# Retention and two MLPs on one core: absolute decays under one causal mask, four transposes in place of four loads, and a new order

## The chip, the cores and the metric

The kernel runs on one core of a Trainium2 chip. The metric is the device time of one execution in microseconds (us), the median of several. Smaller is better.

## What is computed

`q`, `k` and `v` have 2 batches, 8 heads, 768 tokens and 64 features per head. A decaying state runs over the tokens, and its output goes through two MLPs with 512 features in and out and 2048 in between.

```python
gamma = 1.0 - 2.0 ** (-5.0 - np.arange(H))
for t in range(S):
    state = gamma * state + k[t] (outer) v[t]
    y[t] = 1/sqrt(D) * q[t] @ state
x = y, as (1536 tokens, 512)
h = x @ w_in
g = (a0 + a1*h + a2*h**2 + a3*h**3) / (1 + |b0|*|h| + |b1|*h**2 + 1e-6)
x = g @ w_out
h = x @ w_in2
out = (h * sigmoid(h)) @ w_out2
```

## The kernel before

The host lays the data out first. `qt` and `kt` hold `q` and `k` with the features on the partitions, `k` and `v` hold them with the tokens on the partitions, and `consts` and `decays` hold powers of gamma.

**Chunks.** The retention is cut into 12 chunks of 128 tokens (2 batches times 6 positions; chunk c has position c // 2 and batch c % 2). For each chunk `attention` loads qT, kT, vn and kn (256 KB each) and does the following. TensorE forms the scores from kT and qT (`sc`). VectorE multiplies them by a mask (`am`). TensorE multiplies the masked scores by vn (`outs`), and from position 1 on adds qT times the running state `bd` to the same bank. `grow` forms kn times vn, which is added to `bd`. ScalarE and VectorE split the output into a high part `xh` and a low part `xl`. The decay within a chunk lies in the mask `msk` (512 KB, one matrix of 128 x 128 for each head, already causal). The decay between chunks lies in kn, which is multiplied by a power of 1/gamma (`cst`), and in qT, which from position 1 on is multiplied by a power of gamma (`gq`, loaded) after the scores have been taken.

**MLPs.** Four chunks make one group of 512 tokens; there are three groups. A step multiplies a group by 128 columns of w_in (12 matmuls of 512 columns, `mm_in`), runs a chain of elementwise operations on ScalarE and VectorE, splits the result into `gh` and `gl`, and multiplies by 128 rows of w_out (four times 3 matmuls, `mm_out`). The first steps belong to the first group and the first MLP, and run while chunks 4 to 11 are still in work. The weights are loaded raw (512 KB each, a ring of three `raw` buffers), rebuilt by two ScalarE operations and one VectorE operation into `wt`, and split into high and low parts `ih`, `il` (w_in) and `oh`, `ol` (w_out), the high one on ScalarE and the low one on GpSimd. Further groups use the weights in SBUF or load them back from a spill.

**Order.** Every operation is recorded with the cells that it reads and writes (`op`). `Flow.order` then emits all of them in the order that the table `ORDER` (a packed list of numbers) lists, so each engine's queue and the one DMA queue on SP hold what that table says. Engines and queues run in that order and wait on semaphores. The numbers in `R` were used to find orders; a few of them set other things, such as which chunks' scaling runs on VectorE (`kd`, `scp`: chunks 0 to 3) and which on GpSimd.

**Helpers.** Most elementwise operations are recorded by `act`, `tt`, `stt` and `ts`, so all have the lines of those helpers, and the operation is told by its tiles. Loads and stores are recorded by `dma`.

Of the kernel before, what the change touches and what calls it, by code (L numbers as in the profile page):

```python
# [15 lines left out]
AF = mybir.ActivationFunctionType  # L16
ALU = mybir.AluOpType

P = 128
# [4 lines left out]
R = {'lw': -463.92, 'T0': 689.59, 'tau0': 13.93, 'tau1': 122.19, 'c0': -129.63, 'dc': 67.51, 'conv': 39.61, 'half': 427.29, 'absl': -34.77, 'raw': 455.03, 'ret': 752.06, 'spl': -417.39, 'hi': 301.24, 'lo': 31.56, 'inn': -277.93, 'later': -32.81, 'split': -554.53, 'out': 359.39, 'evac': -363.13, 'qload': -20.08, 'scl': 238.79, 'sc': 858.37, 'am': -44.15, 'gr': 112.48, 'av': -547.62, 'bd': 198.47, 'xh': -201.14, 'xl': 110.32, 'glp': 48, 'lop1': 24, 'lop2': 30, 'scp': 4, 'ps': 17, 'ksc': 103.89, 'qa': -467.29, 'ka': 0, 'late': 20, 'mid': 4, 'pev': -317.29, 'pld': -385.01, 'cg': -489.85, 'wm': 11, 'mk': 26.43, 'ck': 21.3, 'g2': (1, 0, 2), 'ch0': 269.21, 'ch1': -102.81, 'ch2': 64.3, 'ch3': 22.33, 'ch4': -52.46, 'ch5': 5.42, 'ch6': -78.23, 'ch7': 237.84, 'ch8': 90.06, 'ch9': -61.88, 'ch10': -106.39, 'ch11': -212.52, 'ru0': 218.22, 'lu0': -107.8, 'ru1': 40.68, 'lu1': -106.06, 'ru2': 91.09, 'lu2': 146.01, 'ru3': -37.17, 'lu3': -39.51, 'rhalf': 125.38, 'wsum': 20.0, 'kd': 4, 'hb': 20}  # L24
# [7 lines left out]
    'c-jru0~-+L8UWDO@0VM)wrp!*aoNVQ?G_f6ZQHiBY}>Z6g{`{xSDfcWgQ$Q2a15fu50D5F0|P+>hzyY+BE*DP5F27ZTu2UaAPO9Z6L1oe!cIsJ=^',  # L32
    'zPYgM5%5_Cp592n8TBB!FG88<Ign_z_aT9!LpUAv<J&c(51ZLmEg6r=buOhF{<($OJjzAf$rSZ~$_^At(X`ArIt*BTyPj!Ou_@DuF;5s0(L7;Xh#',
    'f3(CVjI0NONG8~0^Pz*}Kc{m5TAU70+3Qz?qLRF{%-{310hZ68B7*vA`P!p=dcW_V)AovWP!waYlwV)0}#9q)E4nqrQ39X<5{D7z63S5J$fN1y<U',
    'PEN855GY}AZ!D@p%FBI#?S+P#*5GsuER~Z1x=tS+<<1#93o-B+i(Y7K@@xgZ{ZzWf|wWs+d@0I3+>?^+=urN0XxEF=medi8$`ngP!J1XEbIbZp*z',
    'IG_?Q4cKq2e{MG>$xI*x(gAu3LV;qW*71I6(n^n;HO9TQ_hOoYWS36{mASO)vTAMg|&!4pV_8L$LChJWER^oLLI1qMJl%#6QaGE9!YVtR~&m2e6S',
    'g&|NFdt+=Ih{Iqy6v0v$7b{>Dtc)ozBmRgrF$-43fshFYL00?;|AfIX60%_}tc}?*2j;}S*avgrAp8?YLp`j6^>GyZfpu{(4#$#M9v8znTnbgG8Z',
    'LopkP=70Sjdg3FfF#i*7zH?!8AAyQe#_ekNvR$HpKBT0XkqioCMWzD0ajV*a`DvUd)GiZ~)GLiZ~1>!$g<~jj%CJ#m+b$o8U;CfYWd~&W0}76}w?',
    'm?2a{X4lKu&xB^GvM4Sb)a0brA**FKAV>4`lbD<^n#Cfm=SK(Tmi}P?kF2Do08rR`uT#p-YBhH6ScnQZ~HCl)Zp*k&q8ng&D<3T)xNAWNo!{2ckj',
    'K=j)n^r;t+5nSq2=>Eu(2S<w7F>jv@d_Tn<5-94(kd8>jpzh6q!!eiuHy>0fmd-k)T5Jl3QuEWYDw4dCf>px*bA57VqA)=VFzx-C%6o6;~l(<XK*',  # L40
    'KO!<zIIpJRPm1NZP5zQC9G3fIC}tVQ?nH~NDA;lKD5zvDUFjpuPMKE#bMmUiKGoJo`EHNL@bxCh74J{(VP5$GKvy+@+WFo7=MMQla0XexccEzp|&',
    '#>n&lnS_**&?bmVKhRcqjQjB~oKHqmXg2MDC^V6h(KMPv(I^HbrRfx%V$vi0h@bE?{z%E`CyGU}DGtS@6LgMJP)ce-3n>+)rZg0fPSOl=nnX=0K1',
    'HB^Fbgf93v`~+(jvM@5vd4eqpXyZvQsYF2B+vW<)ETeoVG(c%1wD_F6E_sl%LYm6$+e)5>g}zl$a7wM#?~KC^KcE#Z-(+QVF_7SLqV{N~P#J{Y<5',
# [34 lines left out]
class Cell:  # L78


    bank = None
# [53 lines left out]
def retention_two_mlps(  # L135
# [114 lines left out]


    cst = Buf("cst", [P, NGAM])
    msk = Buf("msk", [P, 2, HP, P])
    gk = cst.t[:].rearrange("p (c h) -> p c h", h=H)
    par = Buf("par", [P, 14])
    ab, na, b1, b0, lb = par.t[:, 0:6], par.t[:, 6:10], par.t[:, 10:11], par.t[:, 12:13], par.t[:, 13:14]
    cq = par.t[:, 11:12]

    cqc, lbc, table = Cell(), Cell(), Cell()

    class Parted:

# [56 lines left out]
    def heads(t):  # L319
        return t[:].rearrange("p (a t) -> p a t", a=HP)  # L320
# [103 lines left out]
    def attention(c, s_banks, o_banks):  # L424
# [13 lines left out]
        if grows:  # L438

            if c < R["ka"]:  # L440

# [498 lines left out]
```

## Time and profile before

| | |
|---|---|
| median of 3 runs | 581.77 us (580.83 to 584.45) |
| profiled execution, its own time | 583.26 us |
| its span in the profile | 581.5 us |
| TensorE matmul busy | 567.3 us, 98% |
| VectorE, ScalarE, GpSimd busy | 427.6, 405.2, 174.2 us |
| DMA | 86.81 MB, mean 149 GB/s |

The span runs from the first to the last instruction of the profiled execution, and all places below are given in us from its start. A busy share is an average over stages with different limits: matmuls are pipelined and their records overlap, so 98% doesn't mean that TensorE is at its peak all the time. What is idle, and what the clock was, is read stage by stage.

### The profile page before, as it was taken

Reading aid. Unit: us, or ns where it says so; the run is one execution under the profiler, and the core shown is the slowest. Engines: PE = TensorE matmul, PEld = TensorE weight load, DVE = VectorE, ACT = ScalarE, POOL = GpSimd, SP = SyncE. Lnnn points to the kernel's source line nnn. Section 1 sums busy time; section 2 is a strip of 40 time slices with the busy share of each in tenths; the row PEclk is TensorE's granted clock in tenths of the full one; section 3 lists DMA queues with packets and bytes.
Section 4 is the critical chain, followed back from the end, with each engine's and each line's share of the span. In section 5 each row is a group of like instructions: output and inputs, shape, how many; then the busy total and the mean of one; then the engine's idle time right before and its main releaser. Section 6 shows DMA issues by size and latency. Waiting matters only on the chain.

```text
span 581.5 us, 8229 instructions
## 1 busy us (share of the span) xinstructions
PE 567.3 (98%) x2902; PEld 467.4 (80%) x2902; DVE 427.6 (74%) x673; ACT 405.2 (70%) x697; POOL 174.2 (30%) x141
## 2 busy tenths in 40 slices
PE   7879999999999999999999999999999999999997
PEld 6767777888888888888888888888888888888885
DVE  3878888798788887798878566578887888663331
ACT  2577988999988887787998888776634545334432
POOL 0435545534644523553463653310000000000000
PEclk8997999999999999999999999999999999999999
DMA  8999856443123310032044667865433422116811
GB/s 299 304 386 312 276 165 235 144 144 112 36 76 106 104 42 20 0 92 90 19 162 147 217 218 246 280 212 167 139 98 108 146 73 91 54 38 207 278 57 73
DMA packets 42585, 86.81 MB, mean 149 GB/s; under 512 B 4656, under 2 KB 4656, under 8 KB 42544
## 3 DMA queue, kind: packets, MB, share of 16 engines
q1 hardware_dynamic: 42544, 86.29, 44.5%
q8 instruction: 23, 0.38, 0.3%
q14 instruction: 18, 0.15, 0.1%
HBM read 65.30 MB, written 20.97 MB: 148 GB/s over the span
## 4 chain that ended last, share of the span: by engine, by line
PE 92%; DMA 3%; ACT 1%; issue 1%; DVE 1%; SPq 1%; POOL 1%; POOLq 0%; DVEq 0%; ACTq 0%
PE acc L603 45%; PE h L550 19%; PE a L550 10%; PE h L766 7%; PE a L766 7%; DMA raw<-in_moe_w_in_dram 2%; PE a L513 1%; DMA qT<-in_qt_dram 1%; PE a L503 1%; PE a L458 1%; SPq L362 1%; PE a L491 1%; PE acc L458 0%; POOL kn L336 0%; ACT wt L328 0%
## 5 line engine op out<-in xcount | busy, mean ns | idle before, releaser
L336 POOL TENSOR_TENSOR gl<-s,gh 128x512 fp32r<-128x512 f32 x48 | 62.7, 1307 | 111.6 <-ACT gh L328 74.8
L603 PE MATMUL acc<-gh,oh 128*128 128x512 f32 x192 | 75.8, 395 | 0.0
L603 PE MATMUL acc<-gl,oh 128*128 128x512 f32 x192 | 74.8, 390 | 0.0
L603 PE MATMUL acc<-gh,ol 128*128 128x512 f32 x192 | 74.8, 389 | 0.0
L603 PE MATMUL acc<-oh,gh 128*128 128x512 f32 x192 | 74.7, 389 | 0.0
L603 PE MATMUL acc<-oh,gl 128*128 128x512 f32 x192 | 74.7, 389 | 0.0
L603 PE MATMUL acc<-ol,gh 128*128 128x512 f32 x192 | 74.7, 389 | 0.0
L550 PE MATMUL h<-xh,ih 128*128 128x512 f32 x168 | 66.3, 395 | 0.0
L550 PE MATMUL h<-xh,il 128*128 128x512 f32 x168 | 65.7, 391 | 0.0
L550 PE MATMUL h<-xl,ih 128*128 128x512 f32 x168 | 65.7, 391 | 0.0
L414 POOL TENSOR_TENSOR il<-wt,ih 128x512 fp32r<-128x512 f32 x36 | 47.1, 1317 | 48.4 <-ACT ih L409 46.2
L343 DVE SCALAR_TENSOR_TENSOR wt<-wt,raw 128x512 int32<-128x512 int32 x64 | 46.2, 732 | 19.9 <-ACT raw L328 12.4
L414 POOL TENSOR_TENSOR ol<-wt,oh 128x512 fp32r<-128x512 f32 x36 | 47.6, 1325 | 29.0 <-ACT oh L409 24.5
L328 ACT ACTIVATE raw<-raw,par 128x512 int32<-128x512 uint32 x64 | 48.3, 759 | 6.1 <-DMA raw<-in_moe_w_in_dram 5.0
L343 DVE SCALAR_TENSOR_TENSOR s<-s,par,h 128x512 f32<-128x512 f32 x65 | 48.2, 744 | 1.2
L328 ACT ACTIVATE wt<-raw 128x512 f32<-128x512 f32 x64 | 42.2, 660 | 6.4 <-DMA raw<-in_moe_w_out_dram 4.0
L603 PEld LDWEIGHTS acc<-gh,oh 128*128 128x128 f32 x192 | 36.0, 188 | 7.8
L603 PEld LDWEIGHTS acc<-oh,gh 128*128 128x128 f32 x192 | 36.0, 188 | 7.5
L603 PEld LDWEIGHTS acc<-gl,oh 128*128 128x128 f32 x192 | 36.0, 188 | 7.5
L603 PEld LDWEIGHTS acc<-oh,gl 128*128 128x128 f32 x192 | 36.0, 188 | 7.5
L603 PEld LDWEIGHTS acc<-ol,gh 128*128 128x128 f32 x192 | 36.0, 188 | 7.4
L328 ACT ACTIVATE gh<-s 128x512 fp32r<-128x512 f32 x56 | 35.0, 626 | 9.9 <-PE acc L603 3.7
(249 smaller groups left out, 1292.0 us busy)
## 6 DMA issues: line engine op xcount, KB each, us to landing
raw<-in_moe_w_out_dram SPq DMA_DIRECT2D x32, 512.0 KB, 4.4
raw<-in_moe_w_in_dram SPq DMA_DIRECT2D x32, 512.0 KB, 4.7
spill<-wt SPq DMA_DIRECT2D x48, 256.0 KB, 4.7
wt<-spill SPq DMA_DIRECT2D x48, 256.0 KB, 2.9
qT<-in_qt_dram SPq DMA_DIRECT2D x12, 256.0 KB, 5.7
kT<-in_kt_dram SPq DMA_DIRECT2D x12, 256.0 KB, 5.9
vn<-in_v_dram SPq DMA_DIRECT2D x12, 256.0 KB, 5.9
kn<-in_k_dram SPq DMA_DIRECT2D x10, 256.0 KB, 6.1
```

Source lines behind the costliest of these rows:

```text
L328: lambda: nc.scalar.activation(out=out_, in_=in_, func=func, **kw),
L336: op(eng, dur, rank, lambda: e.tensor_tensor(out=out_, in0=in0, in1=in1, op=alu), reads, writes, port)
L343: lambda: nc.vector.scalar_tensor_tensor(out=out_, in0=in0, scalar=scalar, in1=in1, op0=op0, op1=op1),
L362: op("swdge" if swdge else "sync", us, rank, lambda: e.dma_start(out=out_, in_=in_), reads, writes)
L414: e.tensor_tensor(out=sl.t[nm + "l"][:, us], in0=wt.t, in1=sl.t[nm + "h"][:, us].bitcast(F32), op=ALU.subtract)
L458: nc.tensor.matmul(heads(sb_[j].t)[:, hp, :], kT.t[js, hp, :], qT.t[js, hp, :], start=True, stop=True)
L491: nc.tensor.matmul(st.t[j * D : (j + 1) * D, hp * D : (hp + 1) * D], kn.t[:, 2 * hp + j, :], vn.t[:, 2 * hp + j, :], start=(hp == 0), stop ...
L503: nc.tensor.matmul(heads(xo.t)[j * D : (j + 1) * D, hp, :], vn.t[:, 2 * hp + j, :], heads(am[j].t)[:, hp, :], start=(hp == 0), stop=not mo ...
L513: nc.tensor.matmul(heads(xo.t)[:, hp, :], old.t[:, hp, :], qT.t[:, hp, :], start=False, stop=True, skip_group_check=True,)
L550: nc.tensor.matmul(h.t, sl.t[w][:, ws], x[g].t[:, c, :], start=(n == 0), stop=(n == 3 * KD - 1))
L603: nc.tensor.matmul(a.t, a1, a2, start=(first and n == 0), stop=(last and n == 2))
L766: nc.tensor.matmul(b_.t, w[0](c, wlo), x[0](c, xlo), start=(start and n == 0), stop=(n == 5), skip_group_check=True)
```

## The change

The decay within a chunk no longer lies in the mask. Scores are now taken from a qT that has already been multiplied by an absolute power of gamma, at position 0 too, and vn, not kn, is multiplied by the power of 1/gamma (in all 12 chunks, before in 10). The mask is then one causal matrix of ones, the same for all heads. It is made on chip from 128 columns of the constants (`cst` grows from 24 KB to 88 KB), and an identity is made from it. The 512 KB load of `msk` is gone. The powers for position 0 come as two rows of 512 numbers, which a matmul with ones spreads over the partitions into the bank `acc3` (`spread`). The six MLP parameters come as two loads into one partition, and a matmul with ones spreads them too (`params`).

For chunks 0 to 3 kT is no longer loaded. TensorE transposes kn (four transposes of 128 x 128, line 448 of the changed kernel) into a score bank, and ScalarE copies the bank to the kT buffer. `ORDER` is a new table over the new list of operations; beyond the first two fifths of TensorE's queue the two orders run alike.

```diff
-    cst = Buf("cst", [P, NGAM])
-    msk = Buf("msk", [P, 2, HP, P])
...
+    cst = Buf("cst", [P, NGAM + P])
+    causal, ident = Buf("causal", [P, P]), Buf("ident", [P, P])
...
-        kT, qT = load(0.0, kTs, kt[b, ci]), load(0.1, qTs, qt[b, ci])
+        turned = c in TURNED
+        kT = kTs() if turned else load(0.0, kTs, kt[b, ci])
+        qT = load(0.1, qTs, qt[b, ci])
...
+            def turn():
+                for hp in range(HP):
+                    nc.tensor.transpose(heads(sb_[1].t)[:, hp, :], kn.t[:, 2 * hp : 2 * hp + 2, :].rearrange("p j d -> p (j d)"), ident.t)
+
+            op("pe", 1.09, rank + R["sc"], turn, [kn, ident], [sb_[1]])
+            act(rank + R["sc"], kT.t[:].rearrange("p a t -> p (a t)"), sb_[1].t, AF.Copy, [sb_[1]], [kT], True)
+
+        gam = gk[:, ci, :].unsqueeze(2).to_broadcast([P, H, D])
+        tt("dve" if c < R["kd"] else "pool", rank - R["ksc"], vn.t, vn.t, gam, ALU.mult, [cst], [vn], bcast=True)
+        if more:
+            gq = shared[ci] if ci in shared else load(0.5, gqs, decays[ci - 1])
+            shared[ci] = gq
+            up = gq.t[:]
+        else:
+            gq = bank["acc3"]
+            up = heads(gq.t)
+        tt("dve" if c < R["scp"] else "pool", rank - R["scl"], qT.t[:], qT.t[:], up, ALU.mult, [gq], [qT], port=more)
...
-                msk.t[:, j, :, :],
+                causal.t[:].unsqueeze(1).to_broadcast([P, HP, P]),
...
-            tt(eng, rank - R["scl"], qT.t[:], qT.t[:], gq.t[:], ALU.mult, [gq], [qT])
...
+    for j in range(2):
+        dma(-60.0 + j, 0.02, rows2[j].t[0:1, :], consts[0:1, NGAM + j * HP * P : NGAM + (j + 1) * HP * P], [], [rows2[j]])
+    dma(-59.0, 0.25, cst.t, consts[:, 0 : NGAM + P], [], [cst])
...
+    def spread():
+        for j in range(2):
+            nc.tensor.matmul(bank["acc3"].t[j * D : (j + 1) * D, :], ones.t[:, 0:D], rows2[j].t[0:1, :], start=True, stop=True)
+
+    def params():
+        nc.tensor.matmul(bank["acc2"].t[:, 0:6], ones.t, pin.t, start=True, stop=True)
```

**The start of TensorE's queue.** Before, after 11 warming matmuls, it holds the scores of chunk 0, its outputs, the scores of chunk 1 and its state (repeated rows left out):

```order
L837 MATMUL h_188<-u_0_164 128x128 x11
L458 MATMUL a_181<-qT_200,kT_203 128x128
L458 MATMUL a_182<-qT_200,kT_203 128x128
...
L503 MATMUL h_188<-am_207,vn_197 64x128
L503 MATMUL h_188<-am_208,vn_197 64x128
...
L458 MATMUL acc_183<-qT_201,kT_204 128x128
L458 MATMUL acc_184<-qT_201,kT_204 128x128
...
L491 MATMUL h_187<-vn_197,kn_194 64x64 x8
```

Now two groups of transposes, the spreading and chunk 0's state stand ahead of chunk 0's scores:

```order
L857 MATMUL h_191<-u_0_167 128x128 x11
L448 MATMUL a_185<-ident,kn_197 128x128 x4
L839 MATMUL acc_189<-t_176,ones 64x512
L839 MATMUL acc_189<-t_177,ones 64x512
L493 MATMUL h_190<-vn_200,kn_197 64x64 x8
L448 MATMUL acc_187<-ident,kn_198 128x128 x4
L468 MATMUL a_184<-qT_203,kT_206 128x128
L468 MATMUL a_185<-qT_203,kT_206 128x128
```

So the first scores have moved behind five other groups, and behind the loads of kn and vn.

**The start of SP's queue**, which holds all loads. Before (qT, kT, vn, kn, cst and msk are the tiles named above, raw the raw weights):

```order
L362 DMA qT_200<-in_qt_dram 128x512
L362 DMA kT_203<-in_kt_dram 128x512
L362 DMA cst<-in_consts_dram 128x48
L362 DMA msk<-in_consts_dram 128x1024
L362 DMA raw_158<-in_moe_w_out_dram 128x1024
L362 DMA vn_197<-in_v_dram 128x512
L362 DMA kn_194<-in_k_dram 128x512
L362 DMA kT_204<-in_kt_dram 128x512
L362 DMA qT_201<-in_qt_dram 128x512
L362 DMA kn_195<-in_k_dram 128x512
L362 DMA raw_156<-in_moe_w_in_dram 128x2x512
```

Now (t are the two rows for `spread`, pin the parameters):

```order
L364 DMA cst<-in_consts_dram 128x176
L364 DMA qT_203<-in_qt_dram 128x512
L364 DMA kn_197<-in_k_dram 128x512
L364 DMA vn_200<-in_v_dram 128x512
L364 DMA t_177<-in_consts_dram 1x512
L364 DMA kn_198<-in_k_dram 128x512
L364 DMA t_176<-in_consts_dram 1x512
L364 DMA qT_204<-in_qt_dram 128x512
L364 DMA kn_199<-in_k_dram 128x512
L364 DMA pin<-in_moe_b_dram 1x2
L364 DMA vn_202<-in_v_dram 128x512
L364 DMA pin<-in_moe_a_dram 1x4
```

The constants and kn have moved to the front, the raw weights behind twelve others, and the four kT, the mask and the wide parameter loads are gone.

**VectorE between steps 0 and 1 and the masks of chunk 6.** Before, from the masks of chunk 5 to the first mask of chunk 6 (`u`, `s`, `t` belong to the elementwise chains of steps 0 and 1):

```order
L336 TENSOR_TENSOR am_207<-a_181,msk 128x512
L336 TENSOR_TENSOR am_208<-a_182,msk 128x512
L343 SCALAR_TENSOR_TENSOR u_0_164<-w_166,par,h_187 128x512
L336 TENSOR_TENSOR s_0_168<-s_0_168,h_187 128x512
L343 SCALAR_TENSOR_TENSOR s_0_168<-s_0_168,par,h_187 128x512
L336 TENSOR_TENSOR bd_193<-a_181,bd_193 64x4x64 x2
L336 TENSOR_TENSOR xl_70<-a_182,xh_67 128x4x128
L343 SCALAR_TENSOR_TENSOR wt_160<-wt_160,raw_156 128x512
L343 SCALAR_TENSOR_TENSOR s_1_169<-s_1_169,par,h_188 128x512
L336 TENSOR_TENSOR am_207<-a_181,msk 128x512
```

Now, over the same stretch:

```order
L338 TENSOR_TENSOR am_211<-a_185,causal 128x512
L338 TENSOR_TENSOR am_210<-a_184,causal 128x512
L338 TENSOR_TENSOR s_1_172<-s_1_172,h_191 128x512
L345 SCALAR_TENSOR_TENSOR s_1_172<-s_1_172,par,h_191 128x512
L345 SCALAR_TENSOR_TENSOR u_0_167<-w_169,par,h_190 128x512
L338 TENSOR_TENSOR s_0_171<-s_0_171,h_190 128x512
L338 TENSOR_TENSOR bd_196<-a_184,bd_196 64x4x64
L338 TENSOR_TENSOR xl_73<-a_185,xh_70 128x4x128
L338 TENSOR_TENSOR bd_196<-a_184,bd_196 64x4x64
L345 SCALAR_TENSOR_TENSOR s_0_171<-s_0_171,par,h_190 128x512
L345 SCALAR_TENSOR_TENSOR wt_163<-wt_163,raw_159 128x512
L338 TENSOR_TENSOR am_210<-a_184,causal 128x512
```

The make-up is much the same. On TensorE, chunk 5's scores have moved from behind the two first steps to between them; its outputs, chunk 6 and then steps 2 and 3 in one piece follow, where before step 2 was followed by chunk 7's scores and the first matmuls of w_out.

## Rows read from the trace of the kernel before

**Rows 1.** All engines by stretch: stretch, length, busy (count), TensorE clock, DMA share, GB/s

```profile
10.00:20.00 10.00, 8.24 (x112) 6.93 (x112) 7.87 (x12) 4.97 (x9) 2.36 (x2) 0.83 0.98 333
...
40.00:50.00 10.00, 8.04 (x76) 6.80 (x71) 8.55 (x15) 7.02 (x12) 6.12 (x6) 0.73 0.86 308
50.00:60.00 10.00, 10.00 (x53) 8.04 (x53) 8.13 (x13) 8.52 (x15) 5.13 (x4) 0.92 1.00 334
...
150.00:300.00 150.00, 150.00 (x661) 123.64 (x660) 125.30 (x189) 128.06 (x218) 68.11 (x54) 1.00 0.21 69
```

**Rows 2.** TensorE in order of time, 0 to 30 us: start, length, instruction, idle before

```profile
6.45 1.48 PE L458 MATMUL a<-qT,kT 64*128 64x128 f32 x16
10.12 1.60 PE L503 MATMUL h<-am,vn 128*64 128x128 f32 x16 [2.20 <-DMA vn<-in_v_dram]
12.06 2.06 PE L458 MATMUL acc<-qT,kT 64*128 64x128 f32 x16 [0.34 <-DMA qT<-in_qt_dram]
...
17.99 1.16 PE L458 MATMUL a<-qT,kT 64*128 64x128 f32 x16 [0.32 <-DMA qT<-in_qt_dram]
19.08 0.69 PE L491 MATMUL h<-vn,kn 128*64 128x64 f32 x16
21.03 1.10 PE L503 MATMUL h<-am,vn 128*64 128x128 f32 x16 [1.26 <-DMA vn<-in_v_dram]
22.05 1.16 PE L513 MATMUL h<-qT,bd 128*128 128x128 f32 x8
23.14 0.69 PE L491 MATMUL h<-vn,kn 128*64 128x64 f32 x16
...
29.94 0.48 PE L550 MATMUL h<-xh,ih 128*128 128x512 f32 x1
```

**Rows 3.** TensorE in order of time, 46 to 52 us

```profile
46.37 1.97 PE L503 MATMUL a<-am,vn 128*64 128x128 f32 x16
48.27 2.08 PE L513 MATMUL a<-qT,bd 128*128 128x128 f32 x8
50.00 0.77 PE L550 MATMUL h<-xh,ih 128*128 128x512 f32 x1
...
51.43 0.44 PE L550 MATMUL h<-xh,ih 128*128 128x512 f32 x1
51.70 0.39 PE L550 MATMUL h<-xl,ih 128*128 128x512 f32 x1
```

**Rows 4.** Loads issued at 2.12, 9.39, 14.16 and 24.72: KB, us to landing

```profile
msk<-in_consts_dram SPq DMA_DIRECT2D x1, 512.0 KB, 4.9
...
kT<-in_kt_dram SPq DMA_DIRECT2D x1, 256.0 KB, 6.0
...
kT<-in_kt_dram SPq DMA_DIRECT2D x1, 256.0 KB, 3.1
...
par<-in_moe_b_dram SPq DMA_DIRECT2D x1, 1.0 KB, 6.7
```

**Rows 5.** VectorE in order of time, 36 to 47 us

```profile
36.86 0.75 DVE L343 SCALAR_TENSOR_TENSOR u<-w,par,h 128x512 f32<-128x512 f32 x1 [0.55 <-ACT s L328]
37.52 0.68 DVE L336 TENSOR_TENSOR s<-s,h 128x512 f32<-128x512 f32 x1
38.12 1.28 DVE L336 TENSOR_TENSOR am<-a,msk 128x512 f32<-128x512 f32 x2
...
45.63 0.68 DVE L336 TENSOR_TENSOR am<-a,msk 128x512 f32<-128x512 f32 x1
```

**Rows 6.** ScalarE in order of time: step 0's first operation; step 4's weights

```profile
35.49 0.67 ACT L328 ACTIVATE w<-h,par 128x512 f32<-128x512 f32 x1
...
61.60 0.61 ACT L409 ACTIVATE ih<-wt 128x512 fp32r<-128x512 f32 x1
```

**Rows 7.** GpSimd in order of time: the low parts of step 4's weights

```profile
61.26 2.54 POOL L414 TENSOR_TENSOR il<-wt,ih 128x512 fp32r<-128x512 f32 x2 [2.46 <-ACT ih L409]
```

**Rows 8.** TensorE in order of time: step 4 begins

```profile
65.90 0.48 PE L550 MATMUL h<-xh,ih 128*128 128x512 f32 x1
```

More of the change, by code (lines that the diff above doesn't have):

```diff
@@ L23 @@
 UNIT = 512
[L24 removed]
+R = {'lw': -463.92, 'T0': 689.59, 'tau0': 13.93, 'tau1': 122.19, 'c0': -129.63, 'dc': 67.51, 'conv': 39.61, 'half': 427.29, 'absl': -34.77, 'raw': 455.03, 'ret': 752.06, 'spl': -417.39, 'hi': 301.24, 'lo': 31.56, 'inn': -277.93, 'later': -32.81, 'split': -554.53, 'out': 359.39, 'evac': -363.13, 'qload': -20.08, 'scl': 238.79, 'sc': 858.37, 'am': -44.15, 'gr': 112.48, 'av': -547.62, 'bd': 198.47, 'xh': -201.14, 'xl': 110.32, 'glp': 48, 'lop1': 24, 'lop2': 30, 'scp': 4, 'ps': 17, 'ksc': 103.89, 'qa': -467.29, 'ka': 0, 'late': 20, 'mid': 4, 'pev': -317.29, 'pld': -385.01, 'cg': -489.85, 'wm': 11, 'mk': 26.43, 'ck': 21.3, 'g2': (1, 0, 2), 'ch0': 269.21, 'ch1': -102.81, 'ch2': 64.3, 'ch3': 22.33, 'ch4': -52.46, 'ch5': 5.42, 'ch6': -78.23, 'ch7': 237.84, 'ch8': 90.06, 'ch9': -61.88, 'ch10': -106.39, 'ch11': -212.52, 'ru0': 218.22, 'lu0': -107.8, 'ru1': 40.68, 'lu1': -106.06, 'ru2': 91.09, 'lu2': 146.01, 'ru3': -37.17, 'lu3': -39.51, 'rhalf': 125.38, 'wsum': 20.0, 'kd': 4, 'hb': 20, 'turned': (0, 1, 2, 3)}
 L_SCALE = 2.0**-29 * (1.0 - 2.0**-16)
@@ L75 @@
+    '7)L-}`zwbBwwm<NP{+IvjFa4Fj_BS3PA|k&1e+S+=L_~`C=pX#OTZBZ!iFoI6BQzpfMDz%bh#3(pB3?v{h}aR4Bcen^jrbp9CZUM',
 )
@@ L433, in load @@
             return buf
-        kT, qT = load(0.0, kTs, kt[b, ci]), load(0.1, qTs, qt[b, ci])
+        sb_ = [bank[x] for x in s_banks]
+        turned = c in TURNED
+        kT = kTs() if turned else load(0.0, kTs, kt[b, ci])
+        qT = load(0.1, qTs, qt[b, ci])
         vn = load(0.3, vns, v[b, ci])
         kn = load(0.4, kns, k[b, ci]) if grows else None
-        if grows:
-            if c < R["ka"]:
-                def decayed():
-                    for n in range(H):
-                        nc.scalar.activation(out=kn.t[:, n, :], in_=kn.t[:, n, :], func=AF.Copy, scale=gk[:, ci, n : n + 1])
-                op("act", 1.95, rank - R["ksc"], decayed, [cst], [kn])
-            else:
-                gam = gk[:, ci, :].unsqueeze(2).to_broadcast([P, H, D])
-                tt("dve" if c < R["kd"] else "pool", rank - R["ksc"], kn.t, kn.t, gam, ALU.mult, [cst], [kn], bcast=True)
-        sb_ = [bank[x] for x in s_banks]
+        if turned:
+            def turn():
[13 more added lines that the diff above has]
+        tt("dve" if c < R["scp"] else "pool", rank - R["scl"], qT.t[:], qT.t[:], up, ALU.mult, [gq], [qT], port=more)
         def sc():
@@ L477, in attention @@
         old = new = bd[b]
-        if more:
-            gq = shared[ci] if ci in shared else load(0.5, gqs, decays[ci - 1])
-            shared[ci] = gq
-            eng = "dve" if c < R["scp"] else "pool"
-            tt(eng, rank - R["scl"], qT.t[:], qT.t[:], gq.t[:], ALU.mult, [gq], [qT])
         st, xo = bank[o_banks[0]], bank[o_banks[1]]
@@ L829, in retention_two_mlps @@
-    op("act", 0.1, 15.0, lambda: nc.scalar.activation(out=b0, in_=ab[:, 4:5], func=AF.Abs), [], [par])
+    op("dve", 0.1, -50.0, lambda: nc.vector.memset(ones.t, 1.0), [], [ones])
+    first = cst.t[:, NGAM : NGAM + P]
+    op("dve", 0.15, -48.0, lambda: nc.vector.tensor_scalar(out=causal.t, in0=first, scalar1=0.0, scalar2=None, op0=ALU.is_gt, op1=ALU.bypass), [cst], [causal])
+    op("dve", 0.06, -47.0, lambda: nc.vector.tensor_copy(out=ident.t[:, 0:1], in_=causal.t[:, 0:1]), [causal], [ident])
@@ new lines, in retention_two_mlps @@
+    op("dve", 0.2, -46.0, lambda: nc.vector.tensor_tensor(out=ident.t[:, 1:P], in0=causal.t[:, 1:P], in1=causal.t[:, 0 : P - 1], op=ALU.subtract), [causal], [ident])
+    def spread():
[3 more added lines that the diff above has]
+        nc.tensor.matmul(bank["acc2"].t[:, 0:6], ones.t, pin.t, start=True, stop=True)
+    op("pe", 0.9, -45.0, spread, [ones, *rows2], [bank["acc3"]])
@@ L832, in retention_two_mlps @@
+    op("pe", 0.2, -44.0, params, [ones, pa, pb], [bank["acc2"]])
+    ab = bank["acc2"].t
+    op("dve", 0.06, 15.0, lambda: nc.vector.tensor_scalar(out=na, in0=ab[:, 0:4], scalar1=-1.0, scalar2=None, op0=ALU.mult, op1=ALU.bypass), [bank["acc2"]], [par])
+    op("act", 0.1, 15.0, lambda: nc.scalar.activation(out=b1, in_=ab[:, 5:6], func=AF.Abs), [bank["acc2"]], [par])
+    op("act", 0.1, 15.0, lambda: nc.scalar.activation(out=b0, in_=ab[:, 4:5], func=AF.Abs), [bank["acc2"]], [par])
     warm = ew["u2"].bufs[0]
```

109 lines of the change are left out of this document (54 added, 55 removed).

## The prediction

> **What bounds the kernel now.** I read the stretches first. From 150 to 300 us, 661 matmuls fill 150 us, 227 ns each, at full clock [rows 1]; the reader is to see that matmuls of 512 columns stand back to back, with the other engines at half to nine tenths. Such a stretch can only lose. From 10 to 60 us it is different: TensorE is idle for 1.8 us of 10 to 20 and for 2.0 us of 40 to 50, and its granted clock averages 0.83 and 0.73 there, 0.92 after 50 [rows 1]. So I read that start in order of time. The first step of the MLP begins at 29.94 [rows 2]. The third (step 2) begins at 50.00, its first three matmuls take 1.43 us, the next starts 0.27 us later [rows 3]. Three at full rate are 0.68, so the start is worth one at 50.75 at full clock. From there on TensorE hardly waits. Step 4 begins at 65.90 [rows 8], 15.15 us later.
>
> Both orders hold the same matmuls ahead of step 2 (chunks 0 to 6 complete, steps 0 and 1), and again ahead of step 4, apart from the transposes and spreads. So the change is worth what it moves the start of step 2, if nothing behind it stalls. The sum is made in the span of 581.5 us; the 1.76 us around it aren't touched, and the profiled execution's 583.26 lies 1.5 above the median of 581.77. The gain is taken from the median.
>
> **Loads.** 1.5 MB go (the mask, four kT), 64 KB and four tiny loads come, and two parameter loads that wrote 128 partitions go. A load of 256 KB landed 3.1 us after issue with little ahead of it and 6.0 with a full queue, the mask's 512 KB took 4.9 [rows 4]. This is worth time only where a load is what ends a wait; the sum says where.
>
> **From the start to step 0.** Prices, from one start to the next [rows 2]: scores 1.09 (17.99 to 19.08), outputs 1.02 (21.03 to 22.05), the product with the state 1.09 (22.05 to 23.14), `grow` 0.69. No row shows a transposition. The four of a chunk move 512 columns through the whole array, as the state product does: 1.09. The bounds are `grow`'s 0.69, also 512 columns, and the doubled 2.08 of a state product at half clock [rows 3]. The spread is two matmuls of 512 columns, each into half the array, like a chunk's outputs: 1.02.
>
> TensorE is free at 6.45, where chunk 0's scores began [rows 2]. Then: transposes of chunk 0 to 7.54, spread 8.56, chunk 0's grow 9.25, transposes of chunk 1 10.34, scores 11.43, the parameters' matmul 11.5, scores of chunk 1 12.6. Chunk 0's two masks on VectorE take 1.28 [rows 5] from 11.43, so its outputs run from 12.7 to 13.7, and the third set of transposes to 14.8. The fourth needs kn of chunk 3 in a buffer that chunk 0's grow frees at 9.25. By rows 4 it lands between 12.4 and 15.3; with the mask and 512 KB of raw weights gone from the loads ahead I take it to be there at 14.8. From here TensorE's own work sets the pace: one set of transposes, four outputs, three scores, three state products, four grows: 1.09 + 4.08 + 3.27 + 3.27 + 2.76 = 14.5. **Step 0 begins at 29.3**, against 29.94. So four sets of transposes eat nearly all that the loads give: 4.4 us of TensorE in a stretch which then has no idle time to hide it.
>
> Two added waits are in that stretch. Chunk 1's scores stand behind the parameters' matmul, whose load may land at 6.7 us [rows 4] from an issue near 5.5, so 12.2: 0.7 late, or nothing. VectorE's scaling of chunk 2's vn stands ahead of chunk 0's masks and waits for a load of the same age: again 0 to 0.8. I take nothing for both and keep 1 us for the range. The four kT copies are 2.4 us of ScalarE, and the mask and identity some 0.4 us of VectorE; ScalarE is half idle from 10 to 20 [rows 1], so they cost nothing. Scaling qT now stands ahead of the scores; for chunks 0 and 1 it runs under the transposes of chunk 1, later it is done a chunk ahead. GpSimd gets two more vn to scale, late, where it isn't waited for.
>
> **From step 0 to step 2.** Step 0 (12 x 0.227 = 2.72), scores of chunk 5 (1.09) and step 1 end 6.53 after step 0 began. Chunk 5's outputs, state product and grow follow, to 9.33. VectorE meanwhile takes step 1's first operations (ScalarE's first one 0.67 [rows 6], then 0.66 and 0.60 [rows 5]) and is free by 8.5. Then two adds into the state, a split, an operation of the chain and a weight rebuild stand ahead of chunk 6's masks: five at 0.60 and the masks' 1.28 bring 13.6. Outputs and state product of chunk 6: **step 2 begins 15.7 after step 0, at 45.0**. Before, that took 20.06 us. Some 2.3 of the difference is the clock: outputs and state product took 1.90 and 1.73 at half clock, for 1.02 and 1.09, and the three matmuls 0.75 more [rows 3]. The rest is order: step 0's chain began on VectorE 6.9 us after step 0 did (36.86), and chunk 6's masks, behind it, were finished at 46.3 [rows 5]; now that chain can begin beside step 1.
>
> 50.75 less 45.0 is 5.75. One correction: step 0's operation on VectorE began 0.70 us after ScalarE's result (36.16 by rows 6, 36.86 by rows 5), released by a later one. I take one such wait off: **5.0 us, 576.8 us**.
>
> **After step 2.** Step 4's weights were ready at 63.80 [rows 7], 2.1 ahead of the matmul. ScalarE's new queue holds 21 operations from chunk 6's output to the last high part of these weights (the old one ended at 62.21 [rows 6]): at 0.6 each and one low part on GpSimd (1.25), 13.9 after step 2, with TensorE there 15.15 after. So 1.3 is spare; the range keeps 1 us for a stall here.
>
> **The rivals.**
> (a) The clock falls again. TensorE waits 2.5 us for chunk 6's masks in my sum (from 11.1 to 13.6), and before, a wait of 2.20 stood ahead of outputs that took 1.60 for 1.02 and scores that took 2.06 for 1.09 [rows 2]. For it: the same length. Against it: what goes before is denser than before. The 2.3 us stay: 579.1.
> (b) Transposes are cheaper. Each full matmul of this type leaves two records (four matmuls are x8 [rows 2]); a transposition might need one pass. At 0.55 the fourth set could start at 13.2, if kn has landed, and step 0 at 27.1: up to 2.2 gained, 574.6; with kn at 14.7, 576.1. The Trainium skill ("TensorE: Matmul & The Clock Gate", Terms) says that the transpose mode is four times faster for FP32; a quarter of 1.09 in all four sets would put step 0 near 26.0, 3.3 earlier, if loads let it. No run here shows a transposition.
> (c) The weights of step 2 set its start. Their two raw loads wait for VectorE to free their buffers; in my walk they land near 28 and are ready by 39. If conversions run late by 8 to 10 us, step 2 starts at 47 to 49: 579 to 581, little gained.
> (d) Slower than before: the transposes leave the array at half clock. The place is the first stage, which has become a chain on TensorE. From the second set of transposes to chunk 3's scores stand some 9 to 10 us of work; at half clock, where scores take 2.06 [rows 2], they cost 9 more and step 0 begins at 38: 5.0 - 9 = 4 lost, 585.8. It decides from step 0 later than 34.3. Against it: the sets are 1 us each among other matmuls, and the trace has no idle time longer than 2.20 in that stretch to compare. The Trainium skill ("TensorE: Matmul & The Clock Gate", Part 4: PE-mode transpose) says that full clock doesn't engage for transposes, since they don't count as busy in the same way; if so the sets would act like idle time, and it speaks for (d), or for a part of it.
>
> **How the numbers follow.** Chances: the forecast 0.47 (575 to 578.5), (b) 0.13, (a) 0.22, (c) 0.10, (d) 0.08. About 1%, 5.8 us, is what a measurement of this kernel can tell from no change. The forecast passes that in three of ten of its cases, (b) in most: 0.29 faster. Slower by as much needs more than (d)'s centre or both clocks: 0.06. The rest, 0.65, is within 1%. The range: (b) with the cheapest transposes and no late release, 573.0, to (c) and (d) in part, 582.5.
>
> **What would show it.** Right: scores of chunk 0 near 10 to 11 us, not 6.45; step 0 at 28 to 30; step 2 at 44 to 46 with a wait of 2 to 3 us ahead of chunk 6's outputs and full clock; no wait of TensorE after. Wrong: a set of transposes far from 1.09; the fourth set waiting for kn beyond 15.3; a half clock in 10 to 30 (d) or 40 to 50 (a); step 4 late on its low weights.

## The result and the profile after

The changed kernel takes **584.98 us** (median of 15, 583.87 to 587.12); the kernel before, run beside it, 581.77 (15 runs). The ratio is 1.0055, with a 95% interval of 1.0037 to 1.0073: half a per cent slower, where 576.8 was forecast. The profiled execution has a span of 584.8 us, for 581.5.

The stretches of the changed kernel (stretch, length, busy (count) of TensorE, its weight loads, VectorE, ScalarE and GpSimd, then TensorE's granted clock, DMA share, GB/s) that answer to [rows 1]:

```profile
10.00:20.00 10.00, 8.68 (x131) 7.46 (x130) 8.53 (x15) 7.12 (x16) 1.28 (x1) 1.00 0.95 342
...
40.00:50.00 10.00, 8.84 (x74) 7.64 (x75) 8.78 (x15) 8.36 (x15) 2.53 (x3) 0.83 0.83 292
50.00:60.00 10.00, 10.00 (x81) 7.92 (x79) 8.50 (x13) 8.99 (x16) 6.78 (x7) 1.00 0.66 215
150.00:300.00 150.00, 145.10 (x630) 117.14 (x629) 120.40 (x181) 123.41 (x210) 61.77 (x49) 1.00 0.20 68
```

The start is better: more TensorE work in 10 to 20 and 40 to 50, and a higher clock. But 150 to 300 us, where 661 matmuls stood back to back before, now hold 630. The 31 that are missing are 7.0 us at 227 ns.

TensorE in order of time (start, length, instruction, idle before and its releaser) answers to [rows 2, 3, 8]:

```profile
6.30 1.06 PE L448 MATMUL a<-ident,kn 128*128 128x128 f32 x4
7.33 1.16 PE L839 MATMUL acc<-t,ones 1*64 1x512 f32 x4
8.42 0.69 PE L493 MATMUL h<-vn,kn 128*64 128x64 f32 x16
9.04 0.66 PE L448 MATMUL acc<-ident,kn 128*128 128x128 f32 x4
9.62 1.16 PE L468 MATMUL a<-qT,kT 64*128 64x128 f32 x16
...
13.27 0.66 PE L448 MATMUL acc<-ident,kn 128*128 128x128 f32 x4
13.77 0.60 PE L448 MATMUL a<-ident,kn 128*128 128x128 f32 x4
15.63 0.32 PE L505 MATMUL h<-u,vn 128*64 128x128 f32 x1 [1.26 <-DVE xl L338]
...
28.96 0.50 PE L552 MATMUL h<-xh,ih 128*128 128x512 f32 x1 [0.26 <-DVE xl L338]
...
40.39 1.16 PE L468 MATMUL a<-qT,kT 64*128 64x128 f32 x16 [1.60 <-issue]
42.33 1.12 PE L493 MATMUL a<-vn,kn 128*64 128x64 f32 x16 [0.77 <-DVE am L338]
43.23 1.92 PE L505 MATMUL a<-am,vn 128*64 128x128 f32 x16
45.08 1.16 PE L515 MATMUL a<-qT,bd 128*128 128x128 f32 x8
46.00 0.47 PE L552 MATMUL h<-xh,ih 128*128 128x512 f32 x1
...
61.56 0.47 PE L552 MATMUL h<-xh,ih 128*128 128x512 f32 x1 [0.49 <-ACT h L330]
```

Step 0 begins at 28.96, step 2 at 46.00, step 4 at 61.56: 1.0, 4.0 and 4.3 us ahead of the kernel before. So the gain that was forecast is there at 60 us, and lost later. Where, this table shows: the start of a step's first matmul, from TensorE's timeline (TensorE's orders in the two kernels differ up to step 29 and are the same behind that, and all kernels hold the same matmuls between step 2 and step 44). The kernels below the second line are the experiments.

| kernel | step 2 | 8 | 14 | 20 | 30 | 44 | from 2 to 44 |
|---|---|---|---|---|---|---|---|
| before | 50.00 | 94.25 | 133.94 | 165.35 | 214.31 | 290.81 | 240.8 |
| after | 46.00 | 90.70 | 128.71 | 162.40 | 217.20 | 294.40 | 248.4 |
| e1 old from 8 | 45.29 | 89.99 | 129.01 | 160.38 | 209.34 | 286.06 | 240.8 |
| e8 light copies | 44.32 | 89.04 | 126.91 | 160.38 | 214.29 | 291.76 | 247.4 |
| e9 light chain | 44.80 | 89.49 | 127.52 | 161.21 | 214.03 | 291.00 | 246.2 |
| e11 old from 20 | 43.65 | 88.36 | 126.44 | 160.13 | 212.57 | 289.65 | 246.0 |
| e12 old from 8 to 20 | 45.94 | 90.64 | 129.66 | 161.03 | 213.34 | 290.25 | 244.3 |
| e13 TensorE sorted | 46.01 | 90.73 | 128.92 | 161.40 | 212.86 | 289.75 | 243.7 |
| e14 others sorted | 45.73 | 90.45 | 128.89 | 165.16 | 214.40 | 291.33 | 245.6 |
| e15 both sorted | 43.61 | 88.30 | 127.50 | 158.68 | 209.01 | 286.07 | 242.5 |

The lead is 3.6 us at step 8, 5.2 at step 14, 3.0 at step 20 and gone at step 30. The page's summary of the chain of waits, before and after:

```profile
PE 92%; DMA 3%; ACT 1%; issue 1%; DVE 1%; SPq 1%; POOL 1%; POOLq 0%; DVEq 0%; ACTq 0%
PE 71%; ACT 13%; DVE 9%; issue 3%; DMA 2%; POOL 1%; SPq 0%; ACTq 0%; POOLq 0%; DVEq 0%
```

The chain itself, in order of time (start, us, what):

```profile
128.73 3.05 PE h L552 x12
131.78 0.02 issue
131.80 0.69 ACT w L330
132.49 0.52 ACT oh L411
133.01 0.52 ACT gh L330
133.53 0.68 ACT s L330
134.21 0.02 issue
134.24 0.75 DVE u L345
134.98 0.61 DVE s L338
...
214.46 1.21 DVE xl L338 x2
215.66 0.04 issue
215.71 1.65 PE acc L605 x6
```

From 131.8 to 215.7 us it never touches TensorE: it goes to and fro between ScalarE and VectorE, through one step's chain after the other. TensorE waits at the head of its queue in 100 to 225 us (what waited for what, us, times, longest):

```profile
PE h L552 <- DVE s L345: 1.6, 2, 1.2
PE acc L605 <- DVE xl L338: 1.4, 1, 1.4
PE a L552 <- DVE s L345: 1.2, 1, 1.2
```

The first and the third kind are a step's w_in matmuls (line 552): their bank is still being read by an earlier step's chain, whose last operation on it is `s`. In the second, w_out products wait for `xl`, a split of what an `acc` bank held. The kernel before has no such row. The three rows are 4.2 us of the 7.6 that the stretch from step 2 to step 44 has grown by; the rest was not traced to single waits.

### The profile page after: what moved, and what is told of

Its sections match the earlier page's. It is cut to its first block, busy times and chain, and to the rows that moved or that the text cites. A ratio compares the mean times of both kernels' runs of the same rounds, so it can differ in the third digit from the quotient of the medians.

```text
span 584.8 us, 8285 instructions
## 1 busy us (share of the span) xinstructions
PE 570.2 (98%) x2924; PEld 466.0 (80%) x2924; DVE 432.0 (74%) x679; ACT 408.2 (70%) x701; POOL 178.7 (31%) x143
## 4 chain that ended last, share of the span: by engine, by line
PE 71%; ACT 13%; DVE 9%; issue 3%; DMA 2%; POOL 1%; SPq 0%; ACTq 0%; POOLq 0%; DVEq 0%
PE acc L605 34%; PE h L552 12%; PE a L552 7%; PE h L768 7%; PE a L768 7%; ACT s L330 2%; DVE s L345 2%; DVE u L345 2%; ACT h L330 2%; ACT w L330 2%; ACT u L330 1%; DVE s L338 1%; ACT gh L330 1%; ACT raw L330 1%; DMA raw<-in_moe_w_out_dram 1%
## 5 line engine op out<-in xcount | busy, mean ns | idle before, releaser
L345 DVE SCALAR_TENSOR_TENSOR wt<-wt,raw 128x512 int32<-128x512 int32 x64 | 48.7, 770 | 22.1 <-ACT raw L330 13.8
L605 PEld LDWEIGHTS acc<-gh,ol 128*128 128x128 f32 x192 | 36.1, 188 | 7.5 <-POOL ol L416 0.4
```

The costliest lines, as they stand in the source:

```text
L345: lambda: nc.vector.scalar_tensor_tensor(out=out_, in0=in0, scalar=scalar, in1=in1, op0=op0, op1=op1),
L605: nc.tensor.matmul(a.t, a1, a2, start=(first and n == 0), stop=(last and n == 2))
```

## The experiments

The theories. **Theory 1**: the new order past step 8 costs the lead. **Theory 2**: ScalarE and VectorE are full in any order, and no earlier start can get through them. **Theory 3**: the added copies and scalings cost it. Line numbers differ by a few between these kernels, as the packed table has another length. "Old" is the order of the kernel before, carried over operation by operation.

**e1 and e2: the two halves of the order exchanged.**

```diff
 e1: the changed kernel; e2: the kernel before
-order = own order
+order = own order up to step 8's first matmul, then the other kernel's order
```

> The changed kernel with its own order up to the first matmul of step 8; from there every engine and queue follows the order of the kernel before (the scaling of qT is pulled ahead of its scores). The computation is unchanged. At step 8 the changed kernel is 3.6 us ahead. Theory 1 (the new order past step 8 costs the lead): the lead stays, 577.4 to 578.5 us, and 130 to 217 us lose nothing against the kernel before. Theory 2 (ScalarE and VectorE are full from 50 to 214 us in any order, and an earlier start of TensorE only waits for them later): the lead is used up between steps 14 and 30, 582 to 585. Theory 3 (the added copies and scalings cost it): as theory 2, since the added work is all in here too.

Measured: **577.63 us**, ratio 0.9936 (0.9914 to 0.9959). From step 2 to step 44 it takes 240.8 us, as the kernel before, and 150 to 300 us are full again:

```profile
100.00:150.00 50.00, 49.95 (x261) 41.00 (x260) 40.51 (x62) 48.01 (x83) 20.71 (x17) 1.00 0.38 127
150.00:300.00 150.00, 149.98 (x661) 123.44 (x660) 125.62 (x189) 128.07 (x219) 69.04 (x54) 1.00 0.21 69
```

So theory 1 holds, and 2 and 3 fall: the same work, begun as early, gets through if it stands in the old order. The new order between steps 8 and 29 costs 1.0055 less 0.9936, 1.2% or 6.9 us (by the two intervals, give or take 0.3%). This kernel is also the fastest of all that ran.

> The mirror of the first: the kernel before with its own order up to the first matmul of step 8, from there the order of the changed kernel. Theory 1: the late order costs its 6.5 to 7 us here too, 588. Theory 2: the late orders are worth about the same, 581.8 to 584. Theory 3: no added work is in here, so 581.8.

Measured: 594.18, ratio 1.0225 (1.0198 to 1.0251). The new stretch is slow here too, by more than theory 1 said: 7.8 us go at the change-over, in steps 8 and 9 (from 0.7 ahead of the kernel before at step 7 to 7.1 behind at step 9), and 8.1 between steps 14 and 30.

**e3: the change without the new order.**

```diff
-order = new
+order = old; each chunk's transposes and copy just ahead of its scores, kn loaded where kT was
```

> All of the change but its order: the operations of the changed kernel in the order of the kernel before, with transposes and copies just ahead of each chunk's scores and kn loaded where kT was. Theory 1: the lateness of the start is passed on to the end and nothing else is lost; with four transposes of 0.65 and a kT copy of 0.6 each in the chain ahead of each score, less some waits for loads, step 0 is 0 to 4 us later than before: 582 to 586, and the difference to before at step 8 is that at step 30. Theory 2: the same start, and the lateness of the start shrinks by step 30 if ScalarE is the bound there. Theory 3: the lateness grows by 2 to 4 us after step 8.

Measured: 604.81, ratio 1.0425 (1.0383 to 1.0467). Nearly all of the loss lies ahead of step 8 (step 2 at 65.58, step 8 at 114.50, step 30 at 234.52, step 44 at 312.06, that is 15.6, 20.3, 20.2 and 21.3 behind); from there to step 30 none is added, against theory 3. The size was missed: TensorE waits in 0 to 60 us first for

```profile
PE a L466 <- POOL qT L336: 6.5, 2, 5.7
PE acc L837 <- DVE ones L829: 3.6, 1, 3.6
```

so with the scaling of qT ahead of the scores, and the spreading first, the old start doesn't fit. So the change needs another order at the start than the old one as it was fitted here (other fits weren't tried); the new order past step 8 isn't needed.

**e4, e11 and e12: where in the stretch.**

```diff
-order = new
+e4:  new up to step 14, then old
+e11: new up to step 20, then old
+e12: new up to step 8, old up to step 20, then new
```

> As the first kernel, but the changed kernel's own order holds up to step 14 and the order of before starts there. The changed kernel is 5.2 us ahead at the start of step 14. Theory 1 with the loss in the order past step 14: 576.5 to 578, as the first or better. Theory 1 with the loss prepared between steps 8 and 14 (ScalarE's queue falls behind there: 44.6 us of work done in 100 to 150 against 48.2): 580 to 584, though the first kernel is at 578. Theory 2: as the first, 582 to 585.

Measured: 584.82, ratio 1.0056 (1.0029 to 1.0083). TensorE is 4.9 us ahead at step 14 (129.07) and 1.2 behind at step 20 (166.51). At the change-over some operations are done in one order and not yet in the other, so this could mean a loss prepared earlier, or only that two orders don't fit together there. It told nothing apart.

> The changed kernel in its own order up to step 20, from there the old order; at the change-over the two orders differ in 12 operations (the new one has done the chain of step 18, the old one the weights of steps 20 and 22 instead). If the loss comes from the order past step 20: 577.5 to 580. If it is prepared before (weights behind, chains ahead): 582 to 586, and the old order's first steps after the change-over show the waits.

Measured: 583.21, ratio 1.0034 (1.0015 to 1.0052).

> The reverse: the changed kernel with its own order up to step 8, the old one up to step 20, the new one after. If the loss comes from the order past step 20: 582 to 586. If it is prepared between steps 8 and 20: 577.5 to 580.

Measured: 581.22, ratio 0.9994 (0.9974 to 1.0013). Against e1 these are 0.98% and 0.58%: both halves of the stretch lose. The two add up to more than the whole 1.19%, so part of them can come from the change-over, as in e4: by the table the new order loses 1.4 us between steps 8 and 20 (71.8 for e1's 70.4), and behind step 20 e11 loses 3.8 against e1 though its order is the old one there. e11 lies where a loss prepared ahead of step 20 was expected, e12 between its two cases.

**e5, e6 and e7: single queues or kinds of operations in the old order.**

```diff
-order = new
+e5: from step 8 on, TensorE's queue old, all other queues new
+e6: from step 8 on, the operations that rebuild weights at old places, all others new
+e7: from step 8 on, the operations that rebuild weights at new places, all others old
```

> The changed kernel, and from step 8 on TensorE's queue alone in the order of the kernel before; all other queues keep the new order. In the new order TensorE takes up the w_out products of steps 10 to 15 some 18 to 25 us after their w_in products, in the old one 20 to 30, so it uses up the ready work sooner. Theory 1a (TensorE's new order asks for results too early): the lead of some 4.9 us is kept, 577.5 to 579. Theory 1b (ScalarE and VectorE fall behind through their own queues: in 100 to 140 ScalarE does 35.7 us of work in the new order and 38.4 in the old): TensorE waits for the same operations, 583 to 586.

> The changed kernel, and from step 8 on the operations that rebuild weights (their loads, ScalarE, VectorE and GpSimd operations) at their places in the old order; the MLP's chains, the chunks and TensorE at their places in the new one. In the old order the weights of steps 20 and 21 are begun at 129.5 on ScalarE, in the new one at 137.1, and ScalarE waits more in 100 to 120. Theory 1c (the weights' operations, which wait for no chain, fill ScalarE's waits in the old order and come too late in the new one): 577.5 to 580. Theories 1a and 1d (TensorE's order, or the order in which the chains of two steps take turns): 583 to 586.

> The opposite of the one before: chains, chunks and TensorE in the old order from step 8 on, the weights' operations at their places in the new one. Theory 1c: 583 to 586, ScalarE still short of work in 100 to 120. Theories 1a and 1d: 577.5 to 579.

Measured: 593.32 (ratio 1.0212, 1.0188 to 1.0236), 595.90 (1.0266, 1.0235 to 1.0297) and 592.24 (1.0195, 1.0170 to 1.0220). All three are 7 to 11 us slower than even the changed kernel and fit none of the theories 1a to 1d. They show only that the queues of one order fit each other and not another's; they leave open which queue is to blame.

**e8 and e9: less work for ScalarE.**

```diff
 e8, in the weights' high parts:
-activation(out=sl.t[nm + "h"][:, us], in_=wt.t, func=AF.Copy)
+n = 8 if u in (8, 9, 10, 11) else UNIT
+activation(out=sl.t[nm + "h"][:, us][:, :n], in_=wt.t[:, :n], func=AF.Copy)
 e9, in step:
-act(now, u2.t, u2.t, AF.Abs, [], [u2])
+few = 8 if 14 <= s <= 29 else GT
+act(now, u2.t[:, :few], u2.t[:, :few], AF.Abs, [], [u2])
```

> The changed kernel in its own order throughout, but the 16 copies that make the high parts of the weights of steps 16 to 23 work on 8 columns in place of 512 (the rest of these high parts is left as it was, so the output isn't the reference's). That takes some 16 times 0.4, 6.5 us, from ScalarE between 100 and 200 us and shortens no chain. Theory 1c, or any theory in which ScalarE's arrears of work are what TensorE waits for after 140 us: 4 to 8 us come back, 577 to 581. Theories 1a and 1d (the chains take turns badly, each waits for the other engine): at most 2 us come back, 583 to 585.

> The changed kernel in its own order, but ScalarE's second operation on u2 (the absolute value) of steps 14 to 29 works on 8 columns in place of 512, so the output isn't the reference's. That takes 16 times some 0.4, 6.5 us, from ScalarE, as much as the light copies of the run before, but out of the chains themselves, between 131.8 and 215.7 us, where the changed kernel's chain of waits runs over ScalarE and VectorE alone. Theory 1d (each chain waits for the other engine, and the chains' own length sets the pace there): 4 to 7 us come back, 578 to 581. Theory 1e (the places in the two queues set it, and what one operation gives is waited away at the next): at most 2 us, 583 to 585, as with the light copies.

Measured: 585.22 (1.0069, 1.0046 to 1.0091) and 583.51 (1.0043, 1.0022 to 1.0063), beside 1.0055 (1.0037 to 1.0073) of the changed kernel: no difference that these intervals separate (from step 2 to step 44 the profiled e8 is 1.0 us shorter and e9 2.2). The work taken away was a little under the 6.5 expected: ScalarE's busy time in 100 to 300 us fell from 168.0 to 163.0 and 164.0. That speaks against theory 1c: ScalarE's load is not what TensorE waits for. e9 lies where theory 1e has it and speaks against 1d.

**e13, e14 and e15: the queues sorted anew.** By the operation times of the trace, an engine takes one of its next few operations when the first isn't ready. In e13 this moves TensorE's queue alone, by swaps of neighbours. By the trace the w_in products of steps 20, 22, 25 and 26 stand one w_out product earlier than in the changed kernel, that of step 27 one later:

```diff
 TensorE's queue, step 20 (steps 22, 25 and 26 likewise)
-w_out product of step 16
 w_in product of step 20
+w_out product of step 16
```

> The changed kernel with all queues as they are but for twelve places on TensorE between steps 7 and 27, where one operation is moved ahead of the one or two before it, which wait longer for their inputs (a w_out product behind the next ready w_out product, the outputs of chunk 11, or the w_in product of step 20, 22, 25, 26 or 27). Theory 1f (TensorE's head of queue waits while ready work stands behind it, and each such wait delays the chains that start behind it): 4 to 7 us come back, 578 to 581. Theory 1e (the places in ScalarE's and VectorE's queues): their queues are untouched, at most 1 us, 584 to 586.

> The counterpart: TensorE's queue and the loads as in the changed kernel; between steps 8 and 31 the queues of ScalarE, VectorE and GpSimd are sorted anew so that, by the operation times of the trace, an engine takes one of the next three operations when its first one isn't ready. Theory 1e: 3 to 7 us come back, 578 to 582. Theory 1f: at most 1 us, 584 to 587.

> The changed kernel, with the queues of TensorE, ScalarE and VectorE between steps 8 and 31 sorted together, by the operation times of the trace: an engine takes one of the next five operations when its first one isn't ready. GpSimd's queue and the loads stay. If the waits of all three queues at operations that aren't ready are the whole loss: 577 to 579.5, as the kernel with the old order past step 8 (577.6). If something else in the stretch (GpSimd, loads) holds part of it: 580 to 582, about as TensorE's swaps alone (581.3).

Measured: 581.29 (ratio 0.9984, 0.9959 to 1.0008), 583.21 (1.0007, 0.9983 to 1.0031) and **579.18** (0.9953, 0.9931 to 0.9974). Against 1.0055 that is 0.71%, 0.48% and 1.02%, or 4.1, 2.8 and 5.9 us of the 6.9. The stretch of 150 to 300 us in e13, e14 and e15:

```profile
150.00:300.00 150.00, 148.39 (x651) 121.44 (x651) 124.38 (x187) 127.74 (x217) 65.28 (x52) 1.00 0.21 72
```

```profile
150.00:300.00 150.00, 147.64 (x649) 121.25 (x648) 125.24 (x187) 126.16 (x215) 64.85 (x50) 1.00 0.21 72
```

```profile
150.00:300.00 150.00, 149.17 (x657) 122.61 (x656) 125.68 (x188) 128.64 (x220) 69.57 (x53) 1.00 0.21 71
```

Of the 31 missing matmuls 21, 19 and 27 are back. e15 lies in the case where the waits are the whole loss, and its interval overlaps that of e1. So the cause is shown but for about 1 us, which these intervals don't tell from nothing: in the new order the engines stand at an operation that isn't ready while ready work waits behind it. How the loss is shared between TensorE and the other engines isn't shown, since each of the three gains is known to some 0.3%; e13 and e14 both lie between the cases of theories 1e and 1f, e13 close to 1f. The old order was not sorted in this way; in the profiled e1 TensorE is idle for 0.02 us of 150 to 300, so there it has next to nothing to win.

**e10: are the transposes worth it?**

```diff
-'turned': (0, 1, 2, 3)
+'turned': ()
-order = new up to step 8, then old
+the same, with kT of chunks 0 and 1 loaded ahead of kn, of chunks 2 and 3 ahead of qT
```

> The first experiment's kernel (new order to step 8, old after), but kT of chunks 0 to 3 is loaded, as in the kernel before, and the four sets of transposes and the four copies are left out. 1 MB more goes through the queue in the first 15 us, some 3.3 us of it at the 300 GB/s of that stretch; TensorE saves 3.0 us of transposes, ScalarE 2.4. If loads set the start of step 2: 1 to 3.5 us later than the first experiment, 578.5 to 581. If the transposes stand on the path as the prediction had it: 575 to 577.6.

Measured: 582.97, ratio 1.0030 (1.0008 to 1.0052), 5.3 us over e1; step 2 begins at 50.38, not 45.29. That is more than the loads alone were thought to cost, and the clock can hold part of it, which wasn't tested apart. The first three stretches:

```profile
0.00:10.00 10.00, 6.71 (x44) 5.59 (x44) 2.85 (x10) 1.58 (x2) 1.19 (x6) 0.94 0.79 265
10.00:20.00 10.00, 7.47 (x100) 6.39 (x98) 5.79 (x11) 3.29 (x8) 0.00 (x0) 0.89 0.95 324
20.00:30.00 10.00, 8.25 (x95) 7.25 (x96) 8.26 (x15) 6.71 (x12) 5.58 (x5) 0.83 1.03 361
```

TensorE is busy for 6.7, 7.5 and 8.3 us of ten and granted less than full clock in each; in e1, with the transposes, it is busy for 8.6, 9.4 and 9.4 and the clock is 1.00. Another place of the four loads was not tried.

## Why the prediction was wrong

**The failed step** is "So the change is worth what it moves the start of step 2, if nothing behind it stalls", with its "1.3 is spare; the range keeps 1 us for a stall here". Behind step 2 stood a stretch of some twenty steps in a new order, and it costs 7.6 us in the profiled executions (248.4 for 240.8), 6.9 by the ratios. The prediction followed ScalarE's queue only to step 4. [Rows 1] were read as a TensorE that "can only lose", and then nothing was put down as lost. How far the new order reaches was known; what it does there was put at nothing without a reason. The warning was in the trace of before, in a stretch that the prediction doesn't use:

```profile
100.00:150.00 50.00, 50.00 (x271) 40.78 (x271) 40.81 (x63) 48.19 (x83) 21.37 (x17) 1.00 0.39 128
```

TensorE has no idle time there and ScalarE 1.8 us in 50. Two engines are full there or nearly so, and the order in which they take turns was replaced. What that would cost could not be read from before; that the stretch had no room to lose in could, and no rival priced it. The time came out within 1% of before, as the largest chance had it, but on the wrong side (the interval of 1.0037 to 1.0073 tells it from no change) and outside the range.

**Right: the start.** With the old order past step 8 the same start gives 577.63, 0.8 over the forecast; by its ratio the gain is 3.7 us, where 5.0 was forecast. Step 0 came at 28.96 (forecast 29.3), step 2 at 46.00 (45.0), step 4 at 61.56, 15.6 behind step 2, where it was 15.2 before, reckoned at full clock [rows 3, 8]; its wait of 0.49 is put down to a chain's operation on ScalarE (`h`), not to its weights. In the executions in which the clock didn't fall (see the last section) step 0 came at 27.5 to 28.7 and step 2 at 43.6 to 44.8, 16.1 behind it (forecast 15.7).

**Mis-sized: the transposes.** 1.09 a set was taken, 4.4 in all. From one start to the next the sets took 1.03, 0.58 and 0.50, and the last one lasted 0.60: 2.7. The first set is the long one: its four matmuls start 0.21 us apart, as those of the warming matmuls just ahead of it do, the matmuls of the later sets 0.11; in e11 the first set, too, lasted 0.60. Rival (b) had that price (0.55), but not its result here: the fourth set began at 13.77, a microsecond ahead of the forecast's 14.8, and then chunk 1's outputs waited 1.26 us for VectorE (`xl`, behind ScalarE's `xh`, which began only at 14.26), a wait that the sum doesn't have. So step 0 came where the dearer sets would have put it: two errors cancel, and that 28.96 lies so near 29.3 is luck. In the 13 executions with this start that wait was 0.48 to 1.34 us. The Trainium skill ("TensorE: Matmul & The Clock Gate", Terms) has the transpose mode four times faster for FP32; the trace agrees with about half the price of the state product that the prediction took (1.09), not with a quarter.

**Rival (a)** came true in part: in the profiled execution the grow of chunk 6 took 1.12 and its outputs 1.92 at half clock, which cost 0.9 us, not 2.3 (see the last section). **Rival (d)** didn't: no fall of the clock is recorded between 0 and 40 us, and step 0 came well ahead of 34.3. The Trainium skill (the same page, Part 4: PE-mode transpose) says that full clock doesn't engage for transposes; here the sets after the first, which stand among other matmuls, ran at 0.50 to 0.60 us each with a clock of 1.00, and e10 without them had the lower clock. **Rival (c)** didn't show: no w_in of steps 2 and 3 waits for a low part.

**Priced at nothing:** the kT copies, the added scalings and the two added waits at the start. e1 holds them all and gains 3.7 us, where 5.0 was forecast, so they were not dear. None of them was tested apart, so that they cost nothing isn't shown.

## What to carry to other kernels

When an edit comes with a new order, the order is an edit of its own, as far as it reaches: find the last place where the two differ, and price that whole stretch, not only the neighbourhood of the edit. The stretch in which TensorE was full and another engine nearly so had no spare in it here, and two orders of the same operations were not equal there. Compare two kernels over the same work (here step 2 to step 44), and try the old order on the part that the edit doesn't need: it was 1.2% here, and single queues of one order put into another made things worse.

## What the runs showed of the hardware

**The clock fell in some executions and not in others, for the same instructions.** Up to step 8 the changed kernel and e1, e4 to e9 and e11 to e15 are the same on every engine. In the profiled executions of six of these 13 the mean clock of 40 to 50 us was 0.83 (step 2 at 45.29 to 46.01), in the other seven 1.00 (43.61 to 44.80). TensorE in e11:

```profile
5.95 0.60 PE L446 MATMUL a<-ident,kn 128*128 128x128 f32 x4
...
38.92 1.16 PE L466 MATMUL a<-qT,kT 64*128 64x128 f32 x16 [1.60 <-issue]
40.86 0.69 PE L491 MATMUL a<-vn,kn 128*64 128x64 f32 x16 [0.77 <-DVE am L336]
41.45 1.09 PE L503 MATMUL a<-am,vn 128*64 128x128 f32 x16
42.48 1.16 PE L513 MATMUL a<-qT,bd 128*128 128x128 f32 x8
43.65 0.47 PE L550 MATMUL h<-xh,ih 128*128 128x512 f32 x1
```

The idle times ahead are the same 1.60 and 0.77 as in the changed kernel, yet the state's grow takes 0.69 for 1.12 and the outputs 1.09 for 1.92, at 2.4 GHz and not at 1.2. So whether the clock falls here is not settled by the instructions alone. From chunk 6's scores to step 2 the six executions took 5.6 to 5.9 us and the seven 4.73, so the fall costs 0.9 to 1.2 us. The two groups' means of step 2 (45.8 and 44.2) lie further apart, because the six were 0.7 us later at those scores already.

What decides it stays open, but one thing goes with it: in the six the first set of transposes lasted 0.98 to 1.06 us, at or near the pace of the warming matmuls ahead of it, in the seven 0.60 to 0.83. The executions in which TensorE came to full pace later at the start are the ones in which the clock fell at 41 to 42 us. With the same instructions, step 2 began anywhere between 43.61 and 46.01, so single profiles of this start can't be compared more closely than that.
